# A four-layer state-space kernel: shift convolution with k as the stationary operand, its product relaid on chip, and layer-one norm statistics tile by tile

## The chip, the cores and the metric

The kernel runs on one core of a Trainium2 chip. The metric is the device time of one execution in microseconds, the median of several runs. The profile that is read below is one execution recorded by the hardware profiler; its span, from the first to the last instruction, is a little shorter than the timed execution.

## The reference, cut to what matters

Two kinds of layer alternate, A B A B, each applied to a layer-normed input and added to its residual. x has 2048 tokens and 640 channels.

```python
def _A_ref(x, ...):                    # a diagonal complex state-space layer
    Bu = x @ B_bar.T                   # 640 states
    h[t] = Lam_bar * h[t-1] + Bu[t]    # recurrence over the 2048 tokens
    return 2 * Re(h @ C.T) + x * Dskip

def _B_ref(q, k, v, shift_k, ssm_k, ssm_D):
    k_shift = sum_t k_pad[:, t:t+S, :] * shift_k[:, 3 - t]   # causal, four taps, per channel
    kv = k_shift * v
    y = fftconv(kv, ssm_k) + kv * ssm_D                      # 2048-long causal convolution per channel
    return q * y

x = x + _A_ref(_layernorm(x), ...)
x = x + _B_ref(_layernorm(x), B_k, B_v, B_shift_k, B_ssm_k, B_ssm_D)
x = x + _A_ref(_layernorm(x), ...)
x = x + _B_ref(_layernorm(x), B_k, B_v, B_shift_k, B_ssm_k, B_ssm_D)
```

k, v and the long kernel ssm_k do not depend on x, and both B layers use the same ones. So the long convolution y is computed once, while the first A layer is being prepared and run, and is read back by both B layers.

## The kernel before

The program is a list of tasks. Each task has an engine (or a choice of ScalarE and VectorE), the tasks it depends on, and a function that emits its instructions. One hand-over string, ORDER, fixes the sequence in which the tasks are emitted; as each engine runs its instructions in the order in which they were emitted, this string is the schedule. A suffix `/a` or `/d` says whether a task with a choice goes to ScalarE (ACT) or to VectorE (DVE). A second table, PLACE, gives every buffer its place in one large SBUF tile (`arena`) and in PSUM (`banks`).

```python
for w in ORDER.split():
    nm, _, e = w.partition("/")
    t = by.pop(nm)
    t.emit({"a": "act", "d": "dve"}[e] if e else t.engs[0])
```

The parts that the change touches are these. For each of five blocks of 128 channels, kv_tasks loads k and v transposed (channels on partitions, tokens along the row), makes the four-tap convolution as four accumulating matmuls with a diagonal stationary operand, multiplies by v on the way out of PSUM and stores the product to a scratch tensor in device memory:

```python
def e_lk(...):                                   # kv_lk: k, transposed by the DMA
    nc.sync.dma_start_transpose(out=kT[:, KPAD:KPAD + L], in_=B_k[0][:, kb * P:(kb + 1) * P])
def e_lv(...):                                   # kv_lv: v, transposed by the DMA
    nc.sync.dma_start_transpose(out=s_vT.get(), in_=B_v[0][:, kb * P:(kb + 1) * P])
for h in range(2):
    def e_mm(...):                               # kv_mm: 8 matmuls of 512 columns
        for b in range(2):
            for l in range(4):
                t0 = KPAD + 1024 * h + 512 * b - l
                nc.tensor.matmul(pk[:, 512 * b:512 * (b + 1)], lhsT=s_ds.get()[:, l, :], rhs=kT[:, t0:t0 + 512],
                                 start=(l == 0), stop=(l == 3))
    def e_ev(...):                               # kv_ev
        nc.vector.tensor_tensor(s_vT.get()[:, sl], s_pk.get(), s_vT.get()[:, sl], ALU.mult)
def e_st(...):                                   # kv_st
    nc.sync.dma_start(out=kvd[kb * P:(kb + 1) * P, :], in_=s_vT.get())
```

For each block of 128 channels, y_pass then does the long convolution as a transform in two stages, for the kernel (K) and for the product (V), a pointwise complex product (`pw`) and the inverse. The V side reads the scratch tensor back in another layout:

```python
def e_vl(_):                                     # yq*_vl
    nc.sync.dma_start(out=s_xv.get(), in_=rows(kvd[c0:c0 + DQ, :]))
```

Its first stage (`KA`, `VA`) uses matmuls on 64 of the 128 rows, in two halves that go to different PSUM banks; the inverse's last stage (`IA`) uses matmuls of 64 columns, each with a stationary operand of its own:

```python
for o4 in range(4):                              # stage A, line 1063
    for h in range(2):
        hs = slice(64 * h, 64 * (h + 1))
        nc.tensor.matmul(pa[:, h, o4, :], lhsT=s_x.get()[hs, 4 * g + o4, :], rhs=T["FA"][hs, :]..., start=True, stop=True)
for u in range(16):                              # IA, line 1190
    nc.tensor.matmul(py[:, u, :], lhsT=TTv[:, 16 * g + u, :], rhs=T["HA"][:], start=True, stop=True)
```

Layer one works on four chunks of 512 tokens (A1c0 to A1c3), each in four tiles of 128 tokens. Its layer norm takes the statistics of a chunk in one VectorE task of four tiles:

```python
def e_bn(_):
    for q in range(4):
        bs = small([P, 2, 6], "bs")
        for h in range(2):
            nc.vector.bn_stats(bs[:, h, :], src(q)[:, h * (D // 2):(h + 1) * (D // 2)])
        nc.vector.bn_aggr(st["mv"][:, q, :], bs[:])
```

After it come, for a chunk, the standard deviation and its reciprocal (`sd`, `post`), the normalised tiles (`id`), a transpose by DMA (`tu`), the input projection (`bp`: lines 635 and 638), its eviction (`ev`), a rotation, the scan and a rotation back on VectorE (`ri`, `sc`, `ro`: the scan is line 674), and the output projection (`cp`: line 726). Layer three (A2) does the same with other statistics. Line 245 is the helper that copies PSUM to SBUF on ScalarE, line 247 the same on VectorE.

Of the kernel before, what the change touches and what calls it, by code (L numbers as in the profile page):

```python
# [17 lines left out]
P = 128  # L18
# [35 lines left out]
    warm yt_io0 kv_kd kv_lk0 kv_dsl yt_io6 a_pl yt_ph0 yt_io12 yt_ph6 a_ldB0 yt_h0 yt_sin0 yt_f0 yt_ph12 a_p0 a_ldB1 kv_k0 kv_d0 yt_sin6 yt_f2 kv_d1 kv_k1  # L54
    yq0_kl a_p1 a_b00:4 kv_d2 a_p2 kv_k2 kv_ds0 yt_sin12 yt_h1 kv_ds4 kv_lv0 a_b01:4 a_b00:0 a_b01:3 a_b0e1:4/a a_p3 kv_ds1 kv_mm0:0 a_wl00:0 a_b0e1:3/a
    yq0_ka yt_neg12 a_b0e0:0/a yt_neg0 a_b00:1 kv_lk1 a_p4 yt_f3 a_b01:1 a_b0e0:4/a yt_f4 a_b0e1:1/a a_b0e0:1/d kv_mm0:1 a_p5 yt_neg6 kv_ev0:0 a_wl00:1
    kv_ds2 yq0_KA:m2 kv_lv1 kv_ev0:1 yq0_KA:m3 yq0_KA:m0 yq0_KA:e2/a a_p6 a_ti a_b00:3 yq0_KA:e0/a a_dd yq0_KA:m1 a_lamd kv_st0 yq0_KA:e1/a kv_mm1:1
    a_b0e0:3/a kv_ds3 a_ta yt_Ci yq0_KA:e3/d kv_mm1:0 kv_ev1:1 a_b00:2 yq0_KB:m3 kv_ev1:0 a_b0e0:2/a yq0_vl a_t0 yq0_KB:e3/a a_b10:4 a_b01:2 a_b0e1:2/a
    yq0_KB:m1 a_b1e0:4/a yq0_KB:m2 a_f yq1_kl yq0_KB:e1/a a_b11:2 yq0_KB:e2/a yq0_KB:m0 a_b1e1:2/a yq0_KB:m4 a_b10:1 yq0_KB:e0/a kv_st1 yq0_VA:m1
    yq0_KB:e4/d a_b1e0:1/a yq0_VA:e1/d yq0_VA:m3 yq0_VA:m2 yq0_VA:e3/a yt_Si a_b11:4 yq0_VA:e2/d a_b11:1 a_b1e1:4/a yq0_VA:m0 a_b1e1:1/a a_b10:0  # L60
    yq0_VA:e0/d a_wc00:0 a_b10:3 a_b10:2 a_b1e0:0/a a_wm00:0 yq0_VB:m0 a_b1e0:3/a a_wl02:0 a_b1e0:2/d yq0_VB:m1 yq0_VB:e0/a yq1_ka kv_lk2 yq1_KA:m2
    yq0_VB:e1/a yq1_KA:m3 yq0_VB:m2 yq1_KA:e2/d yq1_KA:e3/a yq1_KA:m1 yt_nsi yq1_KA:m0 a_wl02:1 yq0_VB:e2/a yq0_VB:m3 yq1_KA:e1/d yq1_KA:e0/a kv_lk3
    yq0_VB:m4 yq0_VB:e3/d a_b01:0 yq0_VB:e4/a yq1_KB:m0 yq0_pw yq1_KB:m3 yq1_KB:e0/a a_wl01:1 yq1_KB:m2 yq1_KB:e3/a yq1_KB:m1 kv_lv2 yq1_KB:e2/a a_b11:0
    yq1_KB:e1/a kv_mm2:0 a_b0e1:0/a a_wl01:0 a_b1e1:0/a yq1_KB:m4 a_wc02:0 a_b11:3 kv_lv3 kv_mm2:1 a_b1e1:3/a yq1_KB:e4/a a_wc00:1 a_wm02:0 yq0_IB:m3
    yq1_vl a_wc01:0 kv_ev2:0 yq0_IB:m2 yq0_IB:e3/a kv_ev2:1 yq0_IB:m1 yq0_IB:e2/a yq2_kl yq0_IB:m0 a_wm01:0 yq0_IB:e1/a yq0_IB:m4 a_wm00:1 kv_mm3:0
    a_wc01:1 yq0_IB:e0/d yq0_IB:e4/a kv_st2 yq1_VA:m1 yq1_VA:m2 kv_ev3:0 yq1_VA:m0 yq1_VA:e1/a yq0_tt yq1_VA:e0/d yq1_VA:e2/a yq1_VA:m3 kv_mm3:1
    yq1_VA:e3/a a_wm01:1 yq2_ka yq1_VB:m4 yq2_KA:m2 kv_ev3:1 yq1_VB:m2 yq1_VB:e4/a yt_h2 yq2_KA:e2/a yq1_VB:m1 yq1_VB:e2/d a_wc02:1 yq1_VB:m0 yq1_VB:e1/a
    yq2_vl yt_h3 yq2_KA:m1 yq1_VB:m3 yq1_VB:e0/d yq2_KA:e1/a yq2_KA:m3 yq1_VB:e3/d yq2_KA:e3/a yq2_KA:m0 kv_lk4 yq0_IA:m1 yq1_pw yq2_KA:e0/a yq0_IA:m0
    yq0_IA:e1/a yq2_KB:m0 yq0_IA:e0/a yq2_KB:m4 yq2_KB:m2 kv_lv4 yq2_KB:e0/a yq2_KB:m1 yq2_KB:e2/a yq2_KB:m3 yq2_KB:e4/a yq2_KB:e1/a yq2_VA:m2 a_wl03:1
    kv_mm4:1 yq2_KB:e3/a a_wl03:0 yq2_VA:e2/a yq2_VA:m1 yq2_VA:m0 a_wl04:1 yq2_VA:e1/a kv_ev4:1 yq1_IB:m1 yq2_VA:e0/a a_wl04:0 yq1_IB:m4 yq1_IB:m2  # L70
    yq1_IB:e1/d yq1_IB:e4/a a_wc03:0 yq3_kl yq1_IB:m0 a_wm02:1 yq1_IB:e2/a yq2_VA:m3 yq1_IB:m3 a_wm03:0 yq1_IB:e0/a yq2_VA:e3/d kv_mm4:0 a_wc04:0 kv_st3
    a_wc03:1 a_wm04:0 yq1_IB:e3/a yq2_VB:m1 kv_ev4:0 a_wl10:1 a_wc04:1 yq2_VB:m0 yq2_VB:e1/a yq3_ka yq2_VB:m2 a_wm03:1 yq1_tt yq2_VB:e0/a a_wm04:1
    yq2_VB:m4 yq2_VB:m3 yq2_VB:e4/a yq2_VB:e2/a a_gm0 yq2_VB:e3/d yq2_pw yq3_KA:m0 yq3_KA:m2 a_wl10:0 a_ge0/a yq3_KA:m1 yq3_KA:e0/a a_gm1 xl0 yq3_KA:e1/a
    yq3_KA:e2/a a_wl11:0 yq1_IA:m1 a_ge1/a yq3_KA:m3 xl1 yq1_IA:m0 a_wc10:0 a_gm4 yq3_KA:e3/a A1c0_ln_bn yq1_IA:e0/a yq4_kl yq1_IA:e1/a yq3_KB:m1 a_ge4/a
    yq2_IB:m1 yq3_KB:e1/a kv_st4 yq2_IB:m3 yq2_IB:e1/a A1c1_ln_bn yq2_IB:m2 A1c0_ln_sd a_wl11:1 yq2_IB:m4 a_gm3 yq3_vl yq2_IB:e4/a yq2_IB:e3/a yq2_IB:e2/a
    A1c0_ln_post yq2_IB:m0 a_wc11:0 a_wm10:0 yq0_st yq3_KB:m4 a_ge3/a yq3_KB:m3 yq4_ka yq2_IB:e0/d a_wc10:1 a_gm2 A1c0_id:3/d A1c1_ln_sd A1c0_id:2/a
    a_wm11:0 yq2_tt yq3_KB:e4/d a_wc11:1 A1c0_id:1/d a_wm10:1 yq3_KB:e3/a A1c1_ln_post yq3_VA:m1 yq3_KB:m0 A1c0_id:0/d a_ge2/a A1c1_id:0/d yq3_VA:e1/a
    yq3_VA:m2 A1c1_id:2/d yq3_KB:m2 yq3_VA:e2/d yq3_KB:e0/a yq3_VA:m0 yq3_KB:e2/d yq3_VA:e0/a yq3_VA:m3 yq4_KA:m0 xl2 yq3_VA:e3/a yq4_KA:e0/d yq4_KA:m3
    yq4_KA:m2 yq4_KA:e3/a yq4_KA:m1 A1c1_id:1/d yq3_VB:m2 yq4_KA:e2/d yq4_KA:e1/a A1c0_tu yq3_VB:m0 yq3_VB:e2/d yq3_VB:m3 yq3_VB:e0/a A1c1_id:3/d
    yq2_IA:m0 yq3_VB:e3/a yq4_KB:m3 A1c2_ln_bn yq2_IA:e0/a A1c1_tu yq4_KB:m0 yq2_IA:m1 yq4_KB:e3/a yq4_KB:m1 yq2_IA:e1/a yq3_VB:m1 yq4_KB:e1/a yq3_VB:m4  # L80
    A1c0_bp:2 a_wl13:0 yq4_KB:e0/d yq3_VB:e4/a yq3_VB:e1/a a_wl12:1 a_wm11:1 A1c2_ln_sd a_t1 A1c2_ln_post yq4_KB:m2 a_wl13:1 yq3_pw A1c0_bp:0 a_wl12:0
    yq4_vl yq2_st A1c0_bp:1 A1c0_ev:2 a_wc13:0 yq4_KB:e2/a a_t2 A1c0_ev:0 a_wl14:0 A1c2_id:1/d a_wc12:0 a_wm13:0 yq1_st A1c2_id:2/d yq3_IB:m3 A1c2_id:0/d
    A1c0_ev:1 yq4_KB:m4 yq3_IB:m0 yq3_IB:e3/a yq4_KB:e4/d yq4_VA:m3 a_wm12:0 yq4_VA:m2 yq3_IB:e0/a a_wl14:1 yq3_IB:m1 A1c0_ri yq4_VA:e2/a yq3_IB:m2
    A1c2_id:3/a A1c1_bp:0 a_wc12:1 A1c2_tu yq3_IB:e1/a a_wc14:0 yq3_IB:e2/a yq4_VA:e3/d a_wc13:1 A1c0_sc yq4_VA:m0 yq4_VA:m1 yq3_IB:m4 yq4_VA:e0/a
    A1c1_bp:2 yq4_VA:e1/a A1c1_ev:0 yq4_VB:m1 A1c1_ev:2 A1c1_bp:1 yq3_IB:e4/d A1c0_cy yq3_tt a_wm14:0 a_wm12:1 a_wm13:1 yq4_VB:e1/a A1c0_ro yq4_VB:m3
    A1c1_ev:1 yq4_VB:m0 yq4_VB:e3/a yq4_VB:m2 xl3 a_wc14:1 yq4_VB:m4 A1c2_bp:0 yq4_VB:e0/a yq4_VB:e4/a yq4_VB:e2/a a_wm14:1 A1c0_xr yq4_pw A1c1_xr
    yq3_IA:m0 A1c2_ev:0 yq3_IA:m1 A1c2_bp:2 yq3_IA:e1/a yq3_IA:e0/a A1c0_cp:2 yq3_st A1c3_ln_bn A1c2_xr yq4_IB:m2 A1c3_xr A1c0_cp:1 yq4_IB:e2/a
    A1c0_xe:2/a A1c1_ri yq4_IB:m4 yq4_IB:m3 A1c0_xe:1/a A1c3_ln_sd A1c0_cp:0 A1c2_ev:2 yq4_IB:e4/a yq4_IB:e3/a A1c1_sc yq4_IB:m1 yq4_IB:m0 yq4_IB:e1/a
    A1c0_cp:3 A1c0_xe:0/a yq4_IB:e0/a A1c3_ln_post A1c3_id:2/a A1c3_id:3/d yq4_tt A1c1_cy A1c1_ro A1c2_bp:1 A1c0_xe:3/a B1c0_ln_nm B1c0_ln_sq:1
    B1c0_ln_sq:2 B1c0_ln_sq:0 A1c3_id:0/d A1c3_id:1/d A1c1_cp:2 A1c2_ev:1 A1c3_tu B1c0_ln_sq:3 A1c2_ri yq4_IA:m1 yq4_IA:m0 yq4_IA:e1/a A1c1_cp:1 A1c2_sc  # L90
    yq4_IA:e0/a B1c0_ln_sd A1c1_xe:2/a yq4_st A1c1_cp:0 A1c1_xe:1/a B1c0_ln_post A1c2_cy B1c0_u:1/a B1c0_u:0/d B1l0 A1c1_cp:3 B1c0_u:2/d B1c0_u:3/a
    A1c2_ro A1c1_xe:0/a B1l1 A1c3_bp:0 A1c1_xe:3/a B2l1 B1c1_ln_nm B1c1_ln_sq:2 B1c0_mm B1c1_ln_sq:3 B1l2 B1c1_ln_sq:1 B1c0_m:0 B1c0_m:3 B1c1_ln_sq:0
    A1c3_bp:2 B1c0_m:2 B1c1_ln_sd B1c1_ln_post B1c0_m:1 B1c1_u:3/a A1c3_bp:1 B1c1_u:0/d A2c0_ln_nm A2c0_ln_sq:0 B1c1_u:1/d B1c1_u:2/d A1c3_ev:0 B1c1_mm
    A2c0_ln_sq:1 B1c1_m:0 A2c0_ln_sq:2 B1c1_m:2 A1c3_ev:2 A1c2_cp:1 B1c1_m:3 A2c0_ln_sq:3 B1c1_m:1 A2c0_ln_sd A2c0_ln_post A2c1_ln_nm A1c3_ev:1
    A2c0_id:0/d A2c0_id:3/d A1c2_cp:0 A1c3_ri A1c2_xe:1/a A2c1_ln_sq:2 A2c1_ln_sq:1 A2c0_id:2/a A2c0_id:1/a A1c2_cp:2 A2c1_ln_sq:0 A1c2_xe:0/d A2c0_tu
    A1c3_sc A2c1_ln_sq:3 A1c2_cp:3 A2c0_bp:1 A1c2_xe:2/d A1c2_xe:3/a A1c3_ro B1c2_ln_nm B1c2_ln_sq:1 B1c2_ln_sq:0 B1c2_ln_sq:2 A2c1_ln_sd A2c0_bp:2
    B1c2_ln_sq:3 A2c1_ln_post B1c2_ln_sd B1c2_ln_post A2c0_bp:0 B1c2_u:1/d B1c2_u:2/a A2c1_id:3/d B1c2_u:0/a A2c1_id:0/d B1c2_u:3/d A2c0_ev:2 B1c2_mm
    A2c0_ev:1 A2c1_id:1/a B1c2_m:2 A2c1_id:2/d A1c3_cp:0 A2c0_ev:0 B1c2_m:3 A2c1_tu B1c2_m:0 B1c2_m:1 A2c0_ri A2c2_ln_nm B1l3 A1c3_cp:3 A1c3_xe:0/a
    A2c2_ln_sq:2 A2c2_ln_sq:1 A2c2_ln_sq:0 A2c0_sc A2c1_bp:0 A2c2_ln_sq:3 A2c2_ln_sd A2c1_bp:1 A2c1_ev:0 A2c0_cy A2c2_ln_post A1c3_xe:3/d A2c2_id:1/a
# [940 lines left out]
def y_pass(S, nc, T, TK, kdst, t_kd, B_ssm_k, kvd, ysd, kv_store, qd):  # L1040
# [79 lines left out]
    def build_V():  # L1120
        s_xv = S.slot(f"{nm}_xv", 32 * DQ, vX)

        def e_vl(_):
            nc.sync.dma_start(out=s_xv.get(), in_=rows(kvd[c0:c0 + DQ, :]))
# [222 lines left out]
```

## Time and profile before

| | |
|---|---|
| time, median of 3 runs | 351.71 us (351.23 to 351.82) |
| span of the profiled execution | 349.0 us |
| TensorE (PE) busy | 325.5 us, 93% |
| VectorE (DVE) busy | 328.5 us, 94% |
| ScalarE (ACT) busy | 241.5 us, 69% |
| GpSimd (POOL) busy | 19.3 us, 6% |
| moved by DMA | 45.91 MB |

A line of the profile's groups gives a source line, an engine and an operation, what is written and read, how often, then the busy time in us and the mean duration of one in ns, and last the idle time of the engine just before, with what ended it. Durations of matmuls contain the time in which the array drains, so a stream of them starts more often than their durations suggest; where the text needs the spacing, it takes the burst's length less one duration, divided by the number of starts after the first. SPq is the instruction queue of SyncE, from which nearly all transfers are issued. A view by stretches gives the busy time of every engine in a part of the span, the TensorE clock (1.00 is full speed) and the mean share of the 16 DMA engines that were busy (it can come out over 1).

### The profile page before, as it was taken

To read this page: it belongs to the slowest core of one execution; us is meant where nothing else is said; L and a number is where in the kernel's file an instruction comes from. 1 tells how busy PE (TensorE), PEld (TensorE's weight loads), DVE (VectorE), ACT (ScalarE), POOL (GpSimd) and SP (SyncE) were. 2 spreads that over 40 slices of the span, in tenths; PEclk is the share of its full clock that TensorE was granted. 3 is DMA by queue.
4 is the path that set the end of the run, shared out by engine and by line. 5 is a ranking of instruction groups with operands and counts; after the bars stand their busy time and mean duration, and the time that the engine had idled before them with its cause. 6 is when DMAs were issued, how large, how long until landed. Compare 5 with 4: busy or idle time off the path is not lost.

```text
span 349.0 us, 8399 instructions
## 1 busy us (share of the span) xinstructions
PE 325.5 (93%) x3533; PEld 246.0 (70%) x3565; DVE 328.5 (94%) x504; ACT 241.5 (69%) x383; POOL 19.3 (6%) x51
## 2 busy tenths in 40 slices
PE   6669998999999999999999999999999999999990
PEld 6437976777686998896776685686868758755550
DVE  8989899898999999999989999999989989999996
ACT  5999998899899999563585598286317727307561
POOL 7590000000000000000000000000000000000000
PEclk9899999999999999999999999999999999999996
DMA  7999999999999977497067800306064040000204
GB/s 221 210 215 219 150 169 234 213 151 223 217 252 190 201 160 135 97 264 230 30 120 123 289 28 2 75 2 153 0 141 162 2 77 0 2 0 3 82 34 188
DMA packets 118712, 45.91 MB, mean 132 GB/s; under 512 B 111629, under 2 KB 112914, under 8 KB 118674
## 3 DMA queue, kind: packets, MB, share of 16 engines
q1 hardware_dynamic: 118528, 45.36, 60.2%
q8 instruction: 28, 0.46, 0.5%
q14 instruction: 10, 0.08, 0.1%
q10 hardware_dynamic: 146, 0.01, 0.0%
HBM read 17.38 MB, written 7.86 MB: 72 GB/s over the span
## 4 chain that ended last, share of the span: by engine, by line
PE 70%; DVE 19%; ACT 5%; DMA 2%; issue 2%; ACTq 1%; DVEq 0%; SPq 0%
PE banks L726 31%; PE banks L635 11%; PE banks L638 11%; PE banks L470 4%; DVE arena L247 4%; ACT arena L245 3%; PE banks L1162 2%; PE banks L1163 2%; PE banks L1025 2%; DMA arena<-in_A_Dskip_dram 1%; DMA arena<-kvd 1%; DVE arena L1141 1%; DVE arena L1140 1%; DVE arena L1139 1%; DVE arena L1138 1%
## 5 line engine op out<-in xcount | busy, mean ns | idle before, releaser
L245 ACT ACTIVATE arena<-banks 128x1024 bf16<-128x1024 f32 (+4 forms) x145 | 120.5, 903 | 37.1 <-PE banks L638 13.3
L726 PE MATMUL banks<-arena 128*128 128x128 bf16 (+1 forms) x859 | 116.5, 290 | 1.1
L726 PEld LDWEIGHTS <-arena 128*128 128x128 bf16 x880 | 67.8, 98 | 48.3
L638 PE MATMUL banks<-arena 128*128 128x256 bf16 x400 | 56.7, 273 | 0.0
L635 PE MATMUL banks<-arena 128*128 128x256 bf16 x400 | 56.7, 273 | 0.0
L674 DVE TENSOR_TENSOR_SCAN arena<-arena 128x1290 bf16<-128x1290 f32 x16 | 44.6, 2832 | 0.2
L638 PEld LDWEIGHTS <-arena 128*128 128x128 bf16 x400 | 39.1, 98 | 4.5
L635 PEld LDWEIGHTS <-arena 128*128 128x128 bf16 x400 | 38.5, 98 | 4.2
L544 ACT ACTIVATE junk<-arena,nmean 128x640 bf16<-128x640 f32 x48 | 39.6, 826 | 1.3
L1087 PE MATMUL banks<-arena 128*128 128x128 bf16 x170 | 35.1, 219 | 0.6 <-ACT arena L245 0.6
L1090 PE MATMUL banks<-arena 128*128 128x128 bf16 x170 | 35.4, 219 | 0.0
L247 DVE CAST arena<-banks 128x1024 bf16<-128x1024 f32 (+3 forms) x29 | 30.2, 1060 | 2.9 <-PE banks L1092 1.1
L1092 PE MATMUL banks<-arena 128*128 128x128 bf16 x150 | 32.8, 219 | 0.0
L1089 PE MATMUL banks<-arena 128*128 128x128 bf16 x150 | 32.8, 219 | 0.0
L589 ACT ACTIVATE arena<-arena,nmr,rstd 128x640 bf16<-128x640 f32 (+1 forms) x26 | 22.7, 912 | 7.4 <-DVE nmr L556 7.4
L539 ACT ACTIVATE nmean<-sums 128x4 f32<-128x4 f32 (+1 forms) x15 | 3.0, 203 | 31.7 <-DVE arena L738 28.2
L1025 PE MATMUL banks<-arena 128*128 128x512 bf16 x74 | 19.6, 397 | 3.4 <-ACT arena L245 2.9
L734 ACT ACTIVATE arena<-banks 128x640 f32<-128x640 f32 x12 | 8.4, 701 | 19.3 <-PE banks L726 19.3
L1162 PE MATMUL banks<-arena 128*128 128x128 bf16 x160 | 19.6, 219 | 0.5 <-ACT arena L245 0.5
L1163 PE MATMUL banks<-arena 128*128 128x128 bf16 x160 | 19.3, 219 | 0.6 <-DVE arena L1143 0.6
L591 DVE TENSOR_SCALAR arena<-arena,rstd,nmr 128x640 bf16<-128x640 f32 (+1 forms) x34 | 17.3, 543 | 0.1
L1087 PEld LDWEIGHTS <-arena 128*128 128x128 bf16 x170 | 16.6, 98 | 1.1
(201 smaller groups left out, 537.5 us busy)
## 6 DMA issues: line engine op xcount, KB each, us to landing
arena<-in_A_x_dram SPq DMA_DIRECT2D x8, 640.0 KB, 5.4
arena<-ysd SPq DMA_DIRECT2D x8, 640.0 KB, 4.9
arena<-in_B_ssm_k_dram SPq DMA_DIRECT2D x5, 512.0 KB, 6.4
kvd<-arena SPq DMA_DIRECT2D x5, 512.0 KB, 7.4
arena<-kvd SPq DMA_DIRECT2D x5, 512.0 KB, 5.1
ysd<-arena SPq DMA_DIRECT2D x5, 512.0 KB, 4.4
out_dram<-arena SPq DMA_DIRECT2D x8, 320.0 KB, 2.2
arena<-in_A_B_re_dram SPq DMA_DIRECT2D x1, 800.0 KB, 6.3
```

The lines of the kernel that those rows point to most:

```text
L245: nc.scalar.activation(out, in_, ACT.Copy)
L247: nc.vector.tensor_copy(out, in_)
L544: nc.scalar.activation(small.junk, src(q), ACT.Square, bias=st["nmean"][:, i:i + 1], scale=1.0, accum_out=st["ssq"][:, i:i + 1])
L635: nc.tensor.matmul(pb[:, jj, c2, :], lhsT=bt1[:, c2, j, k, :], rhs=uT[:, 0:2, k, :], start=(k == 0), stop=False)
L638: nc.tensor.matmul(pb[:, jj, c2, :], lhsT=bt0[:, c2, k, j * P:(j + 1) * P], rhs=uT[:, 2:4, k, :], start=False, stop=(k == NJ - 1))
L674: nc.vector.tensor_tensor_scan(gv, rt, gv, 0.0, ALU.mult, ALU.add)
L726: nc.tensor.matmul(pc[:, o0:o1], lhsT=lh, rhs=rh, start=(n == 0), stop=(n == len(ops) - 1))
L1025: nc.tensor.matmul(pk[:, 512 * b:512 * (b + 1)], lhsT=s_ds.get()[:, l, :], rhs=kT[:, t0:t0 + 512], start=(l == 0), stop=(l == 3))
L1087: nc.tensor.matmul(ps[:, g, 0, :], lhsT=T["Cf"].get()[:, q, :], rhs=are, start=True, stop=single)
L1089: nc.tensor.matmul(ps[:, g, 0, :], lhsT=T["Sf"].get()[:, q, :], rhs=A[:, 2 * q + 1, :], start=False, stop=True)
L1090: nc.tensor.matmul(ps[:, g, 1, :], lhsT=T["NSf"].get()[:, q, :], rhs=are, start=True, stop=single)
L1092: nc.tensor.matmul(ps[:, g, 1, :], lhsT=T["Cf"].get()[:, q, :], rhs=A[:, 2 * q + 1, :], start=False, stop=True)
```

## The change

The change has two parts, and the schedule string and the table of places are new throughout.

**Shift convolution.** k's transposed tile becomes the stationary operand and the diagonal of tap weights the moving one, so the result comes out with tokens on partitions. As the diagonal has nothing outside its two 64 by 64 blocks on the diagonal, each product is taken in two halves of 64 rows and 64 columns, that go to different PSUM banks. v can then be loaded as it lies, without a transpose. The product is written in an order in which one DMA transpose within SBUF gives the layout that the V side wants; the store to device memory and the load from it go.

**Norm statistics.** A chunk's statistics become four tasks, one for each tile, and each may go to VectorE (as before) or to ScalarE, where a sum, a mean and a sum of squares are taken by five activations.

```diff
-        def e_lv(_, kb=kb, s_vT=s_vT):
-            nc.sync.dma_start_transpose(out=s_vT.get(), in_=B_v[0][:, kb * P:(kb + 1) * P])
+        def e_lv(_, kb=kb, s_v=s_v):
+            nc.sync.dma_start(out=s_v.get(), in_=B_v[0][:, kb * P:(kb + 1) * P].rearrange("(a i) d -> i a d", i=P))
 ...
-                for b in range(2):
+                for a in range(8):
                     for l in range(4):
-                        t0 = KPAD + 1024 * h + 512 * b - l
-                        nc.tensor.matmul(pk[:, 512 * b:512 * (b + 1)], lhsT=s_ds.get()[:, l, :], rhs=kT[:, t0:t0 + 512],
-                                         start=(l == 0), stop=(l == 3))
+                        t0 = KPAD + P * (8 * h + a) - l
+                        for r in range(2):
+                            rs = slice(64 * r, 64 * (r + 1))
+                            nc.tensor.matmul(pk[:, 512 * r + 64 * a:512 * r + 64 * (a + 1)], lhsT=kT[rs, t0:t0 + P], rhs=s_ds.get()[rs, l, rs],
+                                             start=(l == 0), stop=(l == 3))
 ...
-                nc.vector.tensor_tensor(s_vT.get()[:, sl], s_pk.get(), s_vT.get()[:, sl], ALU.mult)
+                nc.vector.tensor_tensor(s_kv.get().rearrange("p (r d a) -> p r a d", r=2, a=NT)[:, :, a8, :], s_pk.get().rearrange("p (r a d) -> p r a d", r=2, a=8),
+                                        s_v.get()[:, a8, :].rearrange("p a (r d) -> p r a d", r=2), ALU.mult)
 ...
-            nc.sync.dma_start(out=kvd[kb * P:(kb + 1) * P, :], in_=s_vT.get())
 ...
-            nc.sync.dma_start(out=s_xv.get(), in_=rows(kvd[c0:c0 + DQ, :]))
+            nc.sync.dma_start_transpose(out=s_xv.get(), in_=s_kv.get())
 ...
-    t_bn = S.add(name + "_bn", "dve", 4.1, x_ready, e_bn, uses=uses)
+    for q in range(4):
+        def e_bn(eng, q=q):
+            mv, x = st["mv"], src(q)
+            if eng == "dve":
+                ...                                  # two bn_stats and one bn_aggr, as before
+            else:
+                sm = small([P, 2, 6], "bs")[:, 0, :]
+                nc.scalar.activation(small.junk, x, ACT.Copy, accum_out=sm[:, 0:1])
+                nc.scalar.activation(sm[:, 1:2], sm[:, 0:1], ACT.Copy, scale=-1.0 / D)
+                nc.scalar.activation(mv[:, q, 0:1], sm[:, 0:1], ACT.Copy, scale=1.0 / D)
+                nc.scalar.activation(small.junk, x, ACT.Square, bias=sm[:, 1:2], accum_out=sm[:, 2:3])
+                nc.scalar.activation(mv[:, q, 1:2], sm[:, 2:3], ACT.Copy, scale=1.0 / D)
+        t_bn.append(S.add(f"{name}_bn:{q}", ("dve", "act"), (1.03, 2.3), x_ready, e_bn, uses=uses))
```

Of the 16 statistics tasks the new schedule string sends 4 to ScalarE (one of chunk 0, one of chunk 2, two of chunk 3) and 12 to VectorE. It also changes the engine of other tasks with a choice, which the prediction counts.

## The prediction

> **What bounds the kernel now.** I read first the page's busy times and its span in 40 slices.
>
> ```profile
> PE 325.5 (93%) x3533; PEld 246.0 (70%) x3565; DVE 328.5 (94%) x504; ACT 241.5 (69%) x383; POOL 19.3 (6%) x51
> ...
> PE   6669998999999999999999999999999999999990
> ...
> DVE  8989899898999999999989999999989989999996
> ACT  5999998899899999563585598286317727307561
> ...
> DMA  7999999999999977497067800306064040000204
> ```
>
> Two engines are over 90% busy, so no single sum decides. In the first 16 slices (140 us) everything is near full, DMA included; later ScalarE and DMA have room. Next, the same by stretches, cut where layer one's scans of chunks 0, 1 and 3 begin (139.63, 170.57 and 218.29 us) and where TensorE's last long run ends (332):
>
> ```profile
> core 0: us, PE busy (x) PEld busy (x) DVE busy (x) ACT busy (x) POOL busy (x), PEclk, DMA share, GB/s
> 0.00:139.63 139.63, 126.10 (x1762) 102.62 (x1774) 130.03 (x234) 127.83 (x168) 19.34 (x51) 0.99 1.01 197
> 139.63:170.57 30.94, 30.78 (x347) 24.95 (x349) 30.02 (x37) 17.67 (x25) 0.00 (x0) 1.00 0.69 175
> 170.57:218.29 47.72, 47.40 (x429) 33.71 (x434) 45.71 (x65) 33.90 (x69) 0.00 (x0) 1.00 0.43 103
> 218.29:332.00 113.71, 113.13 (x942) 80.23 (x951) 109.07 (x143) 55.53 (x109) 0.00 (x0) 1.00 0.22 55
> 332.00:349.00 17.00, 8.06 (x59) 4.50 (x58) 13.69 (x27) 6.59 (x17) 0.00 (x0) 0.84 0.27 104
> ```
>
> From 139.63 to 332 us TensorE idles 1.06 us in 192: that stretch is TensorE's. In the front TensorE idles 13.5 us, VectorE only 9.6, ScalarE 11.8. The chain that ended last agrees: its long pieces from 26 to 76 us are VectorE's, after 136 us nearly all TensorE's, and after 332 VectorE's again, for a tail of 17 us.
>
> ```profile
> 45.26 1.30 DVE arena L1138
> ...
> 73.67 1.30 DVE arena L1142
> ...
> 209.70 7.56 PE banks L726 x58
> 217.31 7.35 PE banks L726 x57
> ```
>
> So work taken from TensorE in the front is worth the front's shortening, and VectorE, the fuller one there, limits that.
>
> **What the Trainium skill says.** "TensorE: Matmul & The Clock Gate", section "Back-to-back issue gap", gives the spacing as N/2.4 + 2.5 ns, with a floor of about 60 cycles for up to 64 columns. The trace agrees. The burst of 32 matmuls of 64 columns spans 1.10 us, the last of them 0.193 of it: 0.907 / 31 = 29 ns each, though each has a new stationary operand of 128x128. The same page, "Part 3: Packing small matmuls — row/col tiling", says that matmuls in different row groups run at once, starting up to about 4 ns apart. Stage A shows it: 16 matmuls of 64 rows and 128 columns span 0.62 us, the last 0.216: 0.404 / 7 = 58 ns for a pair, the first interval longer.
>
> ```profile
> 140.62 0.62 PE L1063 MATMUL banks<-FA,arena 64*128 64x128 bf16 x16
> ...
> 155.90 1.10 PE L1190 MATMUL banks<-HA,arena 128*128 128x64 bf16 x32
> ```
>
> "VectorE: DVE Perf Modes", "The perf-mode tier table", puts a tensor_tensor with a PSUM operand at one element a cycle; the trace has 1215 ns for 1024 elements, so a new output order should not lose a faster mode. "SBUF — State Buffer", "Door 1: The DMA port swizzle", warns of a penalty where successive accesses leave a 16-byte line. The new product is written with a step of 32 bytes; no instruction here shows that, and I leave 1.2 us.
>
> **The change part by part.**
>
> ```profile
> L1025 PE MATMUL banks<-arena 128*128 128x512 bf16 x74 | 19.6, 397 | 3.4 <-ACT arena L245 2.9
> ...
> L569 DVE BATCH_NORM_STATS2 bs<-arena 128x6 f32<-128x320 bf16 x32 | 13.5, 462 | 0.0
> L570 DVE BATCH_NORM_AGGREGATE mv<-bs 128x2 f32<-128x12 f32 x16 | 3.3, 209 | 0.6
> ```
>
> TensorE, convolution. Before: 8 matmuls of 512 columns in a task, at 216 ns (a burst of 8 spans 1.89 us, less 0.380, over 7): 1.73 us, ten tasks, 17.3 us. After: 64 matmuls of 64 rows and 64 columns, 32 pairs. If a pair costs what one matmul of 64 columns does now, 29 ns, a task takes 0.93 us. **TensorE −8.0 us**, all before 95 us.
>
> VectorE. A statistics tile costs 2 x 0.462 + 0.209 = 1.13 us; four leave: −4.5. The letters of the schedule string move more: off VectorE go five normalisations of layer one (0.44 each), one of layer three and one of B (0.61), one output-projection eviction (0.90), net three V-side evictions and some smaller ones; onto it come three evictions of the B tables and three of G0 (0.82 each), one in KA, one in KB, two in IB. Together about −1.8. **VectorE −6.3**, of which −3.6 stand ahead of chunk 3's scan of layer one.
>
> ScalarE. A tile is two passes of 0.83, each with an accumulator read of 0.19, and three small ones of 0.20: 2.64 us, four tiles 10.6; the same moves put on another 4.9. **ScalarE +15.5**, about +10 of it before chunk 1's scan. Its idle time ahead of that is 11.8 + 13.3 = 25 us, so this should fit.
>
> SyncE and DMA:
>
> ```profile
> L1014 SPq DMA_TRANSPOSE arena<-in_B_v_dram x5: 2302/2720/5707, 7.0 to 69.0; - x5
> ...
> L1035 SPq DMA_DIRECT2D kvd<-arena x5: 342/511/3627, 21.4 to 93.0; - x5
> ```
>
> The queue loses five transposes of v (5.7 + 2.3 + 2.8 + 2.3 + 2.7 = 15.9 us), five stores (6.7) and five reloads (0.53 each, 2.7). It gains five plain loads of the reloads' shape (2.7) and five transposes within SBUF of 16 blocks; one of 20 blocks holds the queue 3.4 us, so about 3.0 each, 15. **The queue −7.6 us**, and 5 MB of traffic with device memory go. The chain from product to V side was a store (7.4 us to land) and a load (5.1); it becomes one transpose (4.9 for 20 blocks). That lets the V side start some 7 us sooner after its product, which matters once, for the first block; afterwards engine work hides it.
>
> The sum. I take chunk 3's scan as the mark, because the two schedule strings have the same TensorE work ahead of it but for the convolution, hence the same 113 us of it behind. Ahead of the mark VectorE has 3.6 us less, TensorE 8.0 less. If VectorE keeps its present idle time there (9.6 + 0.9 + 2.0 = 12.5 us), the mark and the end come 3.6 us sooner. If TensorE alone decided, 8.0. VectorE's idle time should shrink a little, as TensorE, the queue and DMA have more room: I choose 1.1 us of the 12.5. That makes 4.7 us, and **351.7 − 4.7 = 347.0 us**. The tail keeps its order of about eleven VectorE instructions, so nothing is gained there.
>
> **The rivals.**
>
> 1. Half-row weight loads do not run side by side, and a pair costs 58 ns as in stage A today. Then a task takes 1.9 us and TensorE gains nothing. For it: each pair needs two loads, and no pair of 64 columns stands in this trace. Against it: loads of 64 rows last 94 ns, those of 128 rows 98, and the latter keep up with 29 ns. The front then gives only VectorE's share and the quicker start: 348 to 350 us.
>
> 2. VectorE's idle time closes, and TensorE decides to the end: the whole 8 us, 343.7. For it: the DMA share of 1.0 in the front eases, and many of the front's stops are short hand-overs. Against it: VectorE and ScalarE are each over 91% busy there already.
>
> 3. ScalarE becomes the bound between 110 and 170 us, where it gets the statistics and loses its slack. From 110 to 139.63 it is busy 29.2 of 29.6 us. For it: +10 us against 25 idle, part of which is start-up. Ahead of chunk 0's scan, though, the string gives ScalarE 3.8 us less, by putting weight work later. It would eat the gain: 350 to 353.
>
> 4. The strided product write takes twice as long: 10 x 1.2 = 12 us more on VectorE, in the front: 355 or more. No instruction here speaks for it.
>
> **Range and chances.** The middle is VectorE's ledger, 347 to 348; the lower end is TensorE's ledger, 343.5; the upper end is rival 3 with little gained, 351.5. Faster by over 2% means under 344.7, which needs nearly all of rival 2: 0.22. Slower by over 2% means over 358.7, which needs rival 4 and more: 0.04. The rest, 0.74.
>
> **What would show it.** Convolution matmuls: a burst of 64 in about 1.1 us, busy near 9 to 10 us for all; 1.9 us a burst is rival 1. The product's VectorE instruction at 1.2 us; 2 us or more is rival 4. The queue's transposes within SBUF of 16 blocks at 3 us. TensorE busy near 317.5, VectorE near 322, ScalarE near 257. TensorE's idle time before chunk 3's scan, 14 us now, should grow to 17 or so while VectorE's stays near 11 to 12; a gain that TensorE's idle time swallows wholly would say that I set VectorE's relief too high. The prediction is wrong if the scans of chunks 0 and 1 do not begin 2 to 5 us sooner, or if TensorE gets new gaps behind them.

## The result, and the profile after

The changed kernel takes 387.95 us (386.83 to 388.74) against 351.76 us before on the same chip: a ratio of 1.103, 95% interval 1.100 to 1.106. The prediction was 347.0 us, with a range from 343.5 to 351.5. It was wrong, and on the side to which it had given a chance of 4%.

The page of the changed kernel, its busy times and rows of its 40 slices (now 9.65 us each):

```profile
PE 333.7 (86%) x4099; PEld 261.1 (68%) x4125; DVE 355.6 (92%) x489; ACT 255.4 (66%) x414; POOL 17.5 (5%) x51
...
PE   7616798449597998999999999999999999999990
...
DVE  8999899999989976999799999997989999999996
...
PEclk9878899768988998999999999999999999999996
```

VectorE was to lose 6 us and has 27 more (355.6 against 328.5). TensorE, which was solid from the eighth slice on, now has holes in the first 16, and there its granted clock is low again and again (0.89 in the mean up to the first scan, 0.99 before). The same by stretches, cut at the same marks as before (scans of chunks 0, 1 and 3, and 17 us ahead of the end):

```profile
0.00:171.18 171.18, 129.86 (x2275) 113.72 (x2281) 157.07 (x228) 127.49 (x171) 17.47 (x51) 0.89 0.79 145
171.18:207.21 36.03, 35.92 (x419) 30.36 (x420) 32.94 (x39) 28.53 (x46) 0.00 (x0) 1.00 0.46 105
207.21:253.67 46.46, 46.14 (x409) 31.98 (x414) 44.68 (x60) 33.19 (x64) 0.00 (x0) 1.00 0.61 156
253.67:369.00 115.33, 114.70 (x949) 81.01 (x960) 107.90 (x141) 60.24 (x121) 0.00 (x0) 1.00 0.20 51
```

The first scan begins at 171.18 us, not 139.63: 31.6 us of the loss lie ahead of it. There VectorE is busy 157.1 us, 27 more than before, while ScalarE has the same 127. From the first scan on the span is 5.4 us longer (214.8 instead of 209.4), with TensorE full in both: a second, smaller loss. The groups of instructions name the first. L1037 is the convolution, L1043 its product, L1073 stage A, L1175 the inverse's first stage, and L246 and L248 copy PSUM to SBUF on ScalarE and VectorE; L571 and L575 are the statistics. Of before, the product and stage A:

```profile
L1031 DVE TENSOR_TENSOR arena<-banks,arena 128x1024 bf16<-128x1024 f32 x10 | 12.0, 1216 | 1.2 <-PE banks L1025 1.1
...
L1063 PE MATMUL banks<-FA,arena 64*128 64x128 bf16 x320 | 13.3, 217 | 3.3 <-ACT arena L245 2.1 <-DVE arena L247 0.6 <-DVE arena L1031 0.5
```

And of the changed kernel:

```profile
L1043 DVE TENSOR_TENSOR arena<-banks,arena 128x1024 bf16<-128x1024 f32 x10 | 44.5, 4516 | 1.4 <-PE banks L1037 1.3
L1073 PE MATMUL banks<-FA,arena 64*128 64x128 bf16 x320 | 17.0, 250 | 21.3 <-DVE arena L1043 10.4 <-DVE s_lam L343 7.8 <-ACT arena L246 2.5
L1037 PE MATMUL banks<-arena 64*128 64x64 bf16 x640 | 14.2, 209 | 3.6 <-DVE arena L1043 3.3 <-ACT arena L246 0.3
L571 DVE BATCH_NORM_STATS2 bs<-arena 128x6 f32<-128x320 bf16 x24 | 10.3, 472 | 0.0
L575 ACT ACTIVATE junk<-arena 128x640 bf16<-128x640 bf16 x4 | 2.9, 736 | 0.0
```

The product (L1043) has the shape it had before, 1024 elements a row and ten instructions, and takes 4.5 us instead of 1.2: 44.5 us instead of 12.0. The last column of the second line shows who pays: stage A's matmuls wait 10.4 us for the product (0.5 before) and 7.8 us for a small VectorE step of the A setup (L343) that stands behind two of the products in VectorE's queue. ScalarE waits in turn for TensorE. Waits ahead of the first scan:

```profile
ACT arena L246 <- PE banks L1073: 13.8, 5, 4.8
ACT arena L246 <- PE banks L1175: 12.5, 5, 4.7
PE banks L1073 <- DVE arena L1043: 10.4, 3, 5.0
```

The relaying itself went as expected: the queue's five transposes within SBUF have a median of 3.1 us.

```profile
L1136 SPq DMA_TRANSPOSE arena<-arena x5: 1853/3122/4379, 28.1 to 163.4; - x5
```

### The profile page after: what moved, and what is told of

The parts are those of the page before. It is cut to its first block, busy times and chain, and to the rows that moved or that the text cites. A ratio compares the mean times of both kernels' runs of the same rounds, so it can differ in the third digit from the quotient of the medians.

```text
span 386.0 us, 9528 instructions
## 1 busy us (share of the span) xinstructions
PE 333.7 (86%) x4099; PEld 261.1 (68%) x4125; DVE 355.6 (92%) x489; ACT 255.4 (66%) x414; POOL 17.5 (5%) x51
## 3 DMA queue, kind: packets, MB, share of 16 engines
HBM read 17.38 MB, written 5.24 MB: 59 GB/s over the span
## 4 chain that ended last, share of the span: by engine, by line
PE 66%; DVE 18%; ACT 7%; issue 4%; DMA 2%; ACTq 1%; DVEq 0%
PE banks L735 28%; PE banks L644 11%; PE banks L647 11%; DVE arena L1043 8%; ACT arena L246 4%; PE banks L1073 2%; PE banks L1097 2%; PE banks L1037 2%; PE banks L1100 2%; PE banks L1174 2%; PE banks L1175 1%; PE banks L1102 1%; PE banks L1099 1%; DMA arena<-arena 1%; DVE arena L248 1%
## 5 line engine op out<-in xcount | busy, mean ns | idle before, releaser
L246 ACT ACTIVATE arena<-banks 128x1024 bf16<-128x1024 f32 (+4 forms) x139 | 119.9, 927 | 62.1 <-PE banks L647 20.2
L735 PEld LDWEIGHTS <-arena 128*128 128x128 bf16 x880 | 67.7, 98 | 48.3
L1043 DVE TENSOR_TENSOR arena<-banks,arena 128x1024 bf16<-128x1024 f32 x10 | 44.5, 4516 | 1.4 <-PE banks L1037 1.3
L248 DVE CAST arena<-banks 128x1024 bf16<-128x1024 f32 (+3 forms) x35 | 33.0, 963 | 10.5 <-PE banks L1102 4.6
L647 PEld LDWEIGHTS <-arena 128*128 128x128 bf16 x400 | 39.2, 98 | 4.5
L644 PEld LDWEIGHTS <-arena 128*128 128x128 bf16 x400 | 38.5, 98 | 4.3
L1097 PE MATMUL banks<-arena 128*128 128x128 bf16 x170 | 36.7, 229 | 4.2 <-DVE arena L1043 3.2
L1100 PE MATMUL banks<-arena 128*128 128x128 bf16 x170 | 37.0, 228 | 2.7 <-DVE arena L852 2.7
L1073 PE MATMUL banks<-FA,arena 64*128 64x128 bf16 x320 | 17.0, 250 | 21.3 <-DVE arena L1043 10.4
L1099 PE MATMUL banks<-arena 128*128 128x128 bf16 x150 | 34.0, 227 | 0.0
L1102 PE MATMUL banks<-arena 128*128 128x128 bf16 x150 | 34.0, 226 | 0.0
L598 ACT ACTIVATE arena<-arena,nmr,rstd 128x640 bf16<-128x640 f32 (+1 forms) x33 | 28.7, 912 | 7.0 <-DVE nmr L557 7.0
L1073 PEld LDWEIGHTS <-arena 64*128 64x128 bf16 x320 | 12.4, 109 | 24.3 <-issue 21.7
L1174 PE MATMUL banks<-arena 128*128 128x128 bf16 x160 | 21.6, 232 | 2.7 <-DVE arena L1043 2.5
L1175 PE MATMUL banks<-arena 128*128 128x128 bf16 x160 | 21.5, 231 | 0.5 <-DVE arena L1155 0.5
```

The source lines that it names most:

```text
L246: nc.scalar.activation(out, in_, ACT.Copy)
L644: nc.tensor.matmul(pb[:, jj, c2, :], lhsT=bt1[:, c2, j, k, :], rhs=uT[:, 0:2, k, :], start=(k == 0), stop=False)
L647: nc.tensor.matmul(pb[:, jj, c2, :], lhsT=bt0[:, c2, k, j * P:(j + 1) * P], rhs=uT[:, 2:4, k, :], start=False, stop=(k == NJ - 1))
L735: nc.tensor.matmul(pc[:, o0:o1], lhsT=lh, rhs=rh, start=(n == 0), stop=(n == len(ops) - 1))
L1043: nc.vector.tensor_tensor(s_kv.get().rearrange("p (r d a) -> p r a d", r=2, a=NT)[:, :, a8, :], s_pk.get().rearrange("p (r a d) -> p r a d ...
L1097: nc.tensor.matmul(ps[:, g, 0, :], lhsT=T["Cf"].get()[:, q, :], rhs=are, start=True, stop=single)
```

## The experiments

Theories. **Main:** the product's write, one lone 2-byte element every 32 bytes, is what costs on VectorE. **Rivals:** its reads, contention with the DMA, the relaying, TensorE's falling clock, or ScalarE. Every ratio below is against the kernel before on the same chip. "Ahead" is the start of the first scan in the profiled execution and "behind" the rest of its span.

| run | us | ratio (95%) | ahead | behind |
|---|---|---|---|---|
| before | 351.8 | 1 | 139.6 | 209.4 |
| after | 387.95 | 1.103 (1.100 to 1.106) | 171.2 | 214.8 |
| e1 ten write patterns | 360.1 | one run | 143.2 | 214.8 |
| e2 contiguous write | 353.2 | 1.003 (1.002 to 1.005) | 136.9 | 214.8 |
| e3 stepped reads | 358.8 | 1.018 (1.014 to 1.023) | 143.4 | 214.8 |
| e4 before + split statistics | 356.1 | 1.010 (1.007 to 1.014) | 145.3 | 209.5 |
| e5 runs of 4 | 358.2 | 1.016 (1.012 to 1.020) | 141.8 | 214.8 |
| e6 runs of 4, full rows | 359.0 | 1.019 (1.015 to 1.023) | 142.4 | 214.8 |
| e7 runs of 4, statistics on VectorE | 360.5 | 1.024 (1.020 to 1.028) | 143.1 | 215.2 |
| e8 e4, statistics on VectorE | 352.7 | 1.001 (0.999 to 1.002) | 141.3 | 209.4 |
| e9 e5, table early | 355.0 | 1.007 (1.003 to 1.010) | 139.1 | 214.8 |
| e10 e9, tables on GpSimd | 359.1 | 1.019 (1.015 to 1.023) | 141.4 | 216.8 |
| e11 e2, light product | 353.6 | 1.004 (1.002 to 1.006) | 134.6 | 215.1 |
| e12 e9, late fillers | 355.5 | 1.008 (1.005 to 1.011) | 139.1 | 214.8 |
| e13 e9, all fillers | 356.5 | 1.010 (1.006 to 1.014) | 138.3 | 214.9 |
| e14 e2, all fillers | 355.3 | 1.007 (1.004 to 1.009) | 137.3 | 214.9 |
| e15 e11, statistics on VectorE | 356.1 | 1.012 (1.006 to 1.017) | 137.0 | 215.6 |

**e1: what about the write costs.** Each of the ten products writes in another pattern; same count, same shapes. (The elements then lie in another order than the next stage reads.)

```diff
-   tensor_tensor(s_kv ... "p (r d a) -> p r a d" [:, :, a8, :], ...)      # step 32 bytes
+   # by (block, half): contiguous; step 4, 8, 16, 32 bytes; runs of 2, 4, 8 elements with jumps of 32 bytes;
+   # write contiguous with PSUM read at a step of 512 bytes; the same with v read at 256 bytes as well
```

> The changed kernel with ten different access patterns in its ten product instructions, same elements and same work; the order of the product is left scrambled, so the output is not the reference's. Theory A, the step of the write is what costs: the cost rises once successive elements no longer share a 16-byte line. 1.2 us contiguous, between 1.2 and 4.5 for steps of 4 and 8 bytes, about 4.5 us for steps of 16 and 32 bytes; runs of 2, 4 and 8 elements with jumps of 32 bytes fall as 1 over the run's length, to near 1.2 us for runs of 8. Theory B, reading v and PSUM in the new pattern costs: every one of the write patterns with contiguous reads takes 1.2 us, and the two with stepped reads take 4 us or more. Theory C, contention with transfers or matmuls: all about 4.5 us whatever the pattern.

| pattern | ns |
|---|---|
| all contiguous | 1211 |
| write, step 4 / 8 / 16 / 32 bytes | 1285 / 2458 / 4755 / 4479 |
| write, runs of 2 / 4 / 8 elements, jumps of 32 bytes | 1218 / 1225 / 1219 |
| read of PSUM at 512 bytes | 1218 |
| read of PSUM at 512 bytes and of v at 256 | 1912 |

Six of the ten in VectorE's timeline (start, length in us): the steps of 16 and of 8 bytes, then the runs of 2 together with the step of 32, then the runs of 8 and of 4:

```profile
26.69 4.75 DVE L1062 TENSOR_TENSOR arena<-banks,arena 128x1024 bf16<-128x1024 f32 x1 [0.65 <-PE banks L1037]
...
32.25 2.46 DVE L1062 TENSOR_TENSOR arena<-banks,arena 128x1024 bf16<-128x1024 f32 x1
...
56.93 5.61 DVE L1062 TENSOR_TENSOR arena<-banks,arena 128x1024 bf16<-128x1024 f32 x2
...
64.03 2.38 DVE L1062 TENSOR_TENSOR arena<-banks,arena 128x1024 bf16<-128x1024 f32 x2
```

With contiguous reads the cost follows the write's step: double at 8 bytes, nearly four times at 16 and 32. Contention is out, as slow and fast patterns stand side by side in the same busy stretch (1.22 us, then 4.48 at once behind it, and 1.5 us later 1.22 twice). And a jump of 32 bytes is not what costs by itself: runs of two elements with the same jump take 1218 ns. What costs is single 2-byte elements that lie 8 bytes or more apart. Why is not settled by these runs.

**e2: the changed kernel with a contiguous write, all else as it is** (the next stage reads the elements in another order than it should).

```diff
-   s_kv.get().rearrange("p (r d a) -> p r a d", r=2, a=NT)[:, :, a8, :]
+   s_kv.get()[:, 1024 * h:1024 * (h + 1)].rearrange("p (r a d) -> p r a d", r=2, a=8)
```

> The changed kernel with the product written contiguously and read exactly as in the change; the relaying that the stepped write did is left out, so the output is not the reference's. Theory A: the product instruction falls from 4.5 to 1.2 us, and with it the time from 388 to near what the rest of my ledger gave, 347 (345 to 351). If the other steps of the ledger are wrong as well (VectorE's idle time, ScalarE as a bound) it lands at 352 to 360. Theory B or C: 4.5 us and 388 as before.

353.2 us: of the 36 us, 34.7 go with the write pattern. Relaying, half rows, statistics and the new order are all still there. But 353.2 is not 347.

**e3: the transposition moved from the write to the reads**, so that the result is the reference's.

```diff
-   out "p (r d a) -> p r a d"[:, :, a8, :],  in "p (r a d) -> p r a d",  v "p a (r d) -> p r a d"
+   out "p (r d a) -> p r d a"[:, :, :, a8],  in "p (r a d) -> p r d a",  v "p a (r d) -> p r d a"
```

> The changed kernel, computing all of the reference, with the loops of the product instruction exchanged: it reads PSUM and v with steps of 256 bytes and writes runs of 8 elements, 16 bytes. Theory A: 1.2 to 1.4 us an instruction and a time like that of the contiguous write, about 347 to 350. Theory B: the instruction stays at 4 us or more and the time near 388.

1.92 us each, 358.8 us. With e1 and e2 it gives a dose line at the first scan. VectorE's extra 7.0 us (ten times 1915 less 1219 ns) put it 6.5 us later than in e2, 8.8 us (e1) 6.3 later, 33.0 us (the changed kernel) 34.3 later. Added VectorE work in the front goes into the time nearly one for one.

**e4 and e8: the statistics alone, in the order of before.** e4 splits them into four tasks with the change's four tiles on ScalarE; e8 has all on VectorE.

```diff
-   A1c0_ln_bn
+   A1c0_ln_bn:3/a A1c0_ln_bn:0/d A1c0_ln_bn:1/d A1c0_ln_bn:2/d    # e4; e8: all /d
```

> The kernel before with the norm statistics as four tasks at the old place of the one, four tiles of 16 on ScalarE as in the change; nothing else. My ledger: VectorE has 4.5 us less, 2.3 of it ahead of chunk 0's scan, ScalarE 10.6 us more. If VectorE bounds the front, 349.5 to 351; if ScalarE's fullness between 110 and 140 us takes it back, 351 to 354. If the norm part had a share in the slowdown it would be 360 or more, which I do not expect.

> The kernel before with only the statistics split into four tasks of four tiles, all on VectorE (nothing of the convolution changed). The same split with four tiles on ScalarE took 356.1. If those 4 us came from ScalarE's load: 352, as the kernel before. If they came from splitting the task: 356.

The split costs nothing (352.7); four tiles on ScalarE cost 3.4 us more (1.0% by the ratios). From 110 to 140 us ScalarE is busy 29.5 to 29.6 of 30 us in both; with the tiles on it the rest of its work comes later, and VectorE's busy time there falls from 29.0 to 25.5 us. So rival 3 of the prediction is real in that order.

**e5 and e9: a version that keeps every part of the change.** The product is written in runs of 4 elements (8 bytes), and the permutation of partitions that this leaves is put into the first-stage table of the V side, made once. e9 differs only in where the three steps for the table stand in the order.

```diff
-   out "p (r d a) -> p r a d"
+   out "p (r g a e) -> p a r g e", e=4;  stage_A(..., FA with its rows permuted)
-   ORDER: ... yq0_KB:e0/a yt_vp yt_v0 yt_v1 yq0_VA:m0 ...                    # e5
+   ORDER: ... yt_vp kv_ev1:1 ... kv_mm1:0 yt_v0 a_ta yt_v1 yt_neg0 ...       # e9
```

> The changed kernel with every part kept (64-row halves of k stationary, relaying by transposes in SBUF, statistics per tile), but the product written to the arena in runs of 4 elements (8 bytes) and its operands read contiguously; the partition order that this needs is made good by permuting the rows of V's first-stage table once. My theory (the lone 2-byte writes at a step of 32 bytes are what costs): the product instruction takes 1.2 us, and the kernel about what the version with a contiguous write took, 353 us (352 to 355). Rival (relaying through SBUF or the order of tasks costs as well): 360 or more with the product at 1.2 us.

> The version with runs of 4 took 358, not 353. Its trace shows a stall that the version itself brought in: the permuted table is made on VectorE behind a chain of 22 small operations, TensorE waits 2.4 us for it at 32 us and ScalarE 3.8 us for TensorE after that. Here the three table steps stand some 8 us earlier in the order; nothing else differs. If that stall was the 5 us: 353 (352 to 354.5), as with the contiguous write. If relaying k and v through SBUF or writing in runs of 4 costs by itself: 356 to 358 as before.

The product took 1.22 us, yet e5 took 358.2. Its waits from 28 to 70 us show why: my own table, made behind a chain of 25 small VectorE operations, held TensorE and through it ScalarE and VectorE (L853 is the table's matmul, L1029 and L1058 the two stages of the transform, L187 and L189 the copies out of PSUM):

```profile
ACT arena L187 <- PE banks L1029: 3.8, 3, 2.2
DVE arena L189 <- PE banks L1058: 3.1, 1, 3.1
...
PE banks L853 <- DVE ident_f L849: 2.3, 1, 2.3
```

e9 gets 3.2 of the 5 us back. At 355.0 it is the best variant here that computes the whole reference with the relaying on chip, and does not beat the kernel before.

**e6: the TensorE saving taken back.**

```diff
-   for r in range(2): matmul(pk[64 columns], lhsT=kT[64 rows], rhs=ds[64 x 64])
+   matmul(pk[128 columns], lhsT=kT[128 rows], rhs=ds[128 x 128])
```

> As the version with runs of 4, but the convolution of each task is 32 matmuls over all 128 rows with 128 columns moving instead of 32 pairs on 64-row halves: TensorE gets back about 0.8 us in each of ten tasks, 8 us in all, all of it before chunk 3's scan. If the 8 us saved are swallowed as idle time in a front that ScalarE and VectorE bound: within 1 us of the version with runs of 4. If TensorE decides there: about 8 us longer, 361.

From its first start to its last, a task's burst at full clock takes 0.92 us with half rows (e5) and 1.73 with full rows, so TensorE has 8 us more work, all in the front. The first scan comes 0.5 us later and the time is 0.8 us longer. The 8 us that the half rows save are swallowed in the front.

**e7, e10, e11 and e15: which engine holds the front?** e7 and e15 put all statistics on VectorE. e10 makes the scaled copies of C on GpSimd. e11 multiplies 128 of each product's 1024 elements and copies v into the rest, so e11 and e15 leave seven eighths of the shift convolution out.

```diff
-   A1c0_ln_bn:3/a                                             # e7, e15: the four /a become /d
+   A1c0_ln_bn:3/d
-   nc.scalar.activation(s_wr1, C, ACT.Copy, scale=F6)         # e10
+   nc.gpsimd.tensor_scalar(s_wr1, C, F6, None, ALU.mult)
-   tensor_tensor(kv[1024], pk[1024], v[1024], ALU.mult)       # e11, e15
+   tensor_tensor(kv[:128], pk[:128], v[:128], ALU.mult); tensor_copy(kv[128:1024], v[128:1024])
```

> As the version with runs of 4, but the statistics of all sixteen tiles on VectorE: ScalarE loses 10.6 us, VectorE gets 4.5 us. If ScalarE bounds the front (97% busy from 35 to 110 us): 350.5 to 353, faster than the version with runs of 4. If VectorE bounds it: 354 to 357.

> As the version with the early table, but the twenty scaled copies of C' (0.82 us each on ScalarE, half of them before 110 us) are made on GpSimd, which is idle there: ScalarE loses 16 us, 11 of them in the front, and VectorE gets nothing. If ScalarE bounds the front: 350 to 351.5. If VectorE bounds it: within 1 us of the early table. If GpSimd is slow at it (over 3 us each) or slows VectorE's instructions: longer.

> As the version with the contiguous write (353.2), but each of the ten products multiplies only 128 of its 1024 elements and copies v into the rest (it leaves seven eighths of the shift convolution out of the result): by an estimate from the 256-element instructions of this trace some 0.6 us instead of 1.22, VectorE 6 us less, 4 to 5 of them before chunk 0's scan; nothing changes on ScalarE or TensorE. If VectorE bounds the front: 348 to 350.5, the line of extra VectorE work against time going on below zero. If ScalarE bounds it: 352.5 to 353.5.

> The version with the light product (128 of 1024 elements multiplied, v copied into the rest: seven eighths of the shift convolution left out of the result; 353.6), and the statistics of all sixteen tiles on VectorE: against the version with the contiguous write ScalarE loses 10.6 us and VectorE 1 us. If the two engines bound the front together: 349 to 351. If ScalarE alone bounds it: 350 or less. If neither does: 353 again.

None was faster than what it was derived from, and for e7 and e15 my expectation was wrong. e7 (ScalarE 8.4 us less busy, VectorE 3.6 more) loses 2.3 us against e5; e15 loses about as much against e11, by the ratios 0.8%. Against e2, e15 has 9.0 us less on ScalarE and 2.0 less on VectorE, and its first scan comes at 137.0 us instead of 136.9. e11 takes 6 us off VectorE and no time. In its profiled execution the first scan came 2.3 us sooner than in e2, but its 20 executions spread from 351.3 to 356.0. e10 doesn't test ScalarE: a copy takes GpSimd 2.27 us instead of ScalarE's 0.84, and VectorE then waits for it, 4.1 us in all.

```profile
L356 POOL TENSOR_SCALAR arena<-arena,s_F 128x640 f32<-128x640 bf16 x20 | 45.3, 2270 | 94.1 <-DMA arena<-in_A_C_im_dram 35.4 <-DVE arena L360 33.4 <-ACT arena L187 14.9
```

So no engine alone holds the front in this order; ScalarE's relief by itself, with nothing moved to VectorE, was not measured. The chain that ended last, summed over its pieces up to the first scan, is 53 us TensorE, 53 VectorE, 18 ScalarE and 9 DMA in before, and 53 TensorE, 35 VectorE, 38 ScalarE and 11 issue in e2. What left VectorE came back as ScalarE's: the chain changes hands, and work taken from one engine lets another piece end last.

**e12, e13 and e14: TensorE's clock.** e2 has a mean clock of 0.974 where before has 0.986: new half-clock stretches of 3.4 us, two more than before in the profiled run. Groups of matmuls that nobody reads are put ahead of TensorE's longest waits.

```diff
-   ... yq4_KA:m2 ... yq4_KA:m1 ...
+   ... fl5 yq4_KA:m2 ... fl6 yq4_KA:m1 ...      # 10 to 20 matmuls of 128 columns each; three groups (e12), seven (e13, e14)
```

> The version with the early table (355.0), with three groups of 10, 18 and 10 small matmuls that nobody reads, put on TensorE just ahead of the three waits of 0.7, 1.2 and 0.7 us between 108 and 114 us. If the half-clock window at 113 us comes from that idle stretch and costs what it is long: the window goes and the time falls by some 1.7 us, to 353.3. If the clock isn't what costs: unchanged or up to 1 us longer.

> As the late fillers, and four more groups of 14 to 20 matmuls ahead of the four longest waits of TensorE between 9 and 24 us (1.1 to 1.7 us each). If the clock decides: two or three more half-clock windows go, mean clock back at 0.986 as in the kernel before, and the time 351 to 352. If the front is bound by ScalarE and VectorE whatever TensorE's clock: as the late fillers alone, within 1 us.

> The version with the contiguous write (353.2; the order of the product's elements is not what the next stage reads) with the same seven groups of filler matmuls. If the clock decides: 350 to 351, below the kernel before. If not: 353 to 354.

The stretch up to e13's first scan, with the clock in the column before the DMA share:

```profile
0.00:138.34 138.34, 123.45 (x2386) 108.07 (x2392) 125.85 (x230) 127.10 (x171) 17.50 (x51) 1.00 1.03 180
```

The clock is at 1.00 throughout, where e9 had 0.94 with three half-clock stretches of 17 us together, and the time is no shorter. So in e9 the half-clock stretches are a symptom and not what costs, as far as the fillers can show it, whose own cost is not separated. e14 shows the same for e2, with one stretch of 3.4 us left. Which gaps bring them stays open: e13 still has gaps of up to 1.8 us between its matmuls in the first 24 us, where e9's are 1.5 at most.

## Why the prediction was wrong, point by point

**The step that failed: "no instruction here shows that, and I leave 1.2 us".** The product's write was mis-sized: 4.5 us each, ten times 3.3 us more, 33 us; with a contiguous write it is gone (e2). The Trainium skill's "VectorE: DVE Perf Modes", section "The perf-mode tier table", was read rightly: with a PSUM operand there is no faster mode to lose, and contiguous it stays at 1211 ns. But that says nothing of a stepped write. The warning in "SBUF — State Buffer", section "Door 1: The DMA port swizzle", was taken up and then priced at nothing. The page asks for at least two accesses to a 16-byte line and has a penalty where each access goes to a new one. Pairs at 32 bytes (1218 ns) and single elements at 16 and 32 bytes (4755 and 4479) agree with that; the step of 8 bytes has two elements in a line and costs double all the same (2458), so the measured pattern decides. Rival 4 had the right instruction, at 1.2 us more instead of 3.3, and its chance came from "No instruction here speaks for it", which is no evidence against it.

**The second step that failed: "If VectorE keeps its present idle time there", with chunk 3's scan as the mark.** Without the write the gain is still absent, and the stretches of e2 show why:

```profile
0.00:136.89 136.89, 121.25 (x2280) 106.06 (x2281) 125.85 (x227) 126.74 (x171) 17.57 (x51) 0.96 0.98 181
136.89:172.91 36.02, 36.02 (x421) 30.36 (x420) 32.95 (x38) 28.55 (x46) 0.00 (x0) 1.00 0.46 105
172.91:219.50 46.59, 46.59 (x415) 32.02 (x414) 44.85 (x61) 33.33 (x65) 0.00 (x0) 1.00 0.63 156
219.50:334.00 114.50, 114.50 (x948) 80.22 (x947) 107.44 (x138) 59.45 (x120) 0.00 (x0) 1.00 0.20 50
```

Chunk 3's scan begins at 219.5 us, 1.2 later than before, and not 4.7 sooner. Ahead of it VectorE is busy 203.6 us instead of 205.8, which is 2.1 less and not 3.6 (4.2 less in the front, 2.0 more behind it), and its idle time, which the prediction held at 11 to 12 us, grew from 12.5 to 15.9. The first scan does come 2.7 us sooner, as the prediction's "2 to 5 us" had it. But chunk 1's comes 2.3 us later, and that alone was to be a sign of being wrong. From the first scan on TensorE has no gap at all, so VectorE's work behind it could not move a mark that lies 82.6 us further on.

What has to be done from the first scan on decides, and that grew by 5.4 us: the column "behind" is 209.4 to 209.5 in all three runs with the order of before, and 214.8 to 215.6 in thirteen of the fourteen with the new one, whatever was changed in the front (in e10 GpSimd's copies hold it up). Of the 5.4 us, 4.5 lie between the first scan and the end of TensorE's last matmul (200.5 us before, 205.0 in e2), and 0.9 in VectorE's tail behind that (8.9 and 9.8), which the prediction had taken as unchanged. The groups of layer one's input product ahead of the first scan, of before:

```profile
L635 PE MATMUL banks<-arena 128*128 128x256 bf16 x67 | 9.6, 273 | 0.0
L638 PE MATMUL banks<-arena 128*128 128x256 bf16 x65 | 9.2, 273 | 0.0
```

and of e2:

```profile
L644 PE MATMUL banks<-arena 128*128 128x256 bf16 x53 | 7.6, 273 | 0.0
L647 PE MATMUL banks<-arena 128*128 128x256 bf16 x50 | 7.1, 273 | 0.0
```

29 fewer stand ahead of it: in the new string a group of 40 of chunk 1's product lies behind chunk 0's scan, and one of 20 ahead of it instead (32 of the 40 had started before it, and 3 of the 20 have now). They start every 109 ns (five in 0.55 us), so 29 are 3.2 us; 16 matmuls of the transform's second stage and the inverse and four pairs of stage A, put off likewise, make it 4.3 of the 4.5. So TensorE does about 12 us less in the front (8 saved, 4.3 put off), and the front is only 2.7 us shorter: −2.7 + 5.4 is the 2.7 us by which e2's span (351.7) exceeds that of before (349.0). That the order does this is read from the strings and traces; the new convolution in the old order was not tried, and why the tail is longer stays open.

**The rest of the list.** Half-row pairs at 29 ns: right, a burst of 64 at full clock takes 1.11 us, 0.92 from its first start to its last; rival 1 is out. TensorE's ledger of −8.0: right (ten bursts, each 0.81 us shorter in e5 than in e6), and worth 0.5 to 0.8 us. Rival 2, TensorE deciding in the front: out, by e6. TensorE busy near 317.5: 326.3 in e2, 333.7 with the write; TensorE's idle time before chunk 3's scan near 17: 15.6 in e2. ScalarE busy near 257: 255.4. Queue transposes near 3 us: right. 5 MB less traffic with device memory: the page shows 2.6 MB less written (5.24 for 7.86) and the same 17.38 read. Rival 3, ScalarE as the bound: true in the old order (e4), while in the new one the tiles are better on ScalarE (e7). VectorE near 322: 324.5 in e2, so its ledger of −6.3 came out as −4.0; 355.6 with the write.

## What to carry to other kernels

Before a transposition is put into the output pattern of a VectorE instruction, measure that very pattern: if neighbouring writes are lone 2-byte elements 8 bytes or more apart, keep a run of at least two elements, or put the step on the reads, which cost less here (1.9 us instead of 4.5, e3). When a kernel has a stretch in which one engine never idles, split the time at its start: ahead of it count what shortens the whole chain, behind it count that engine's work and the tail, and look in the new order for work that crossed the line.

## What was not expected of the hardware

- A VectorE product of 1024 bf16 outputs costs 1211, 1285, 2458, 4755 and 4479 ns at write steps of 2, 4, 8, 16 and 32 bytes, but 1218 ns in pairs with jumps of 32 bytes; with both reads stepped by 256 bytes it costs 1915 (e3).
- The half-clock stretches ahead of the first scan last 3.4 or 6.8 us each. The changed kernel has eight of them, 37.5 us in all, and before has one; e9 has three, and with filler matmuls ahead of TensorE's longest waits none is left (e13).
- GpSimd takes 2.27 us to scale 640 bf16 elements a row (e10), ScalarE 0.84 (e9).
